# A three-layer kernel with eight experts: row sorts, weight chunks and an overflow count in second layers, and another order at the turn to the transform

## The chip, the cores and the metric

The kernel runs on one core of one Trainium2 chip. The metric is the device time of one execution in microseconds. A core has five engines with a queue each: TensorE (PE, with PEld for weight loads), VectorE (DVE), ScalarE (ACT), GpSimd (POOL) and SyncE (SP), which here only issues transfers; semaphores order the engines against each other.

## The reference, cut to what matters

```python
attn = _attn_ref(x, a, B, C)            # chunked scan, (4, 8, 768, 32)
x = attn.transpose(0, 2, 1, 3).reshape(4, 768, 256)
# _moe_ref: each token goes to one expert e, the last one or the best new one
h = np.maximum(x[b, s] @ w1[e], 0.0)    # 256 -> 1024
out[b, s] = p[e] * (h @ w2[e])          # 1024 -> 256
# _moe2_ref
mixed = np.real(np.fft.fft(np.fft.fft(x, axis=1), axis=2))
u = x + mixed
un = (u - u.mean(-1)) / np.sqrt(var + 1e-06)
return u + np.maximum(un @ w_ch1, 0.0) @ w_ch2   # 256 -> 1024 -> 256
```

All is float32; matrices are multiplied as three products of a high and a low part (`w1h`, `w1l`, `xh`, `xl`, `hh`, `hl`).

## The kernel before, in words

The program has three parts on one core. The scan and the choice of experts come first, and scatter each token's row into `xs_buf`, sorted by expert. Then come the experts, and last the transform: mixing (a Fourier transform as matmuls) and a channel layer of six groups of 512 rows, g0 to g5.

The function `experts` runs the experts in order of their load: E0 to E5, then E6 and E7. `CAPS` gives the rows that each may hold (128 and 256 for E0, then 480, 448, 384, 352, 320, 416, 416). E6 and E7 are split by batch, so that the transform can start early: of E6 the first 288 rows run, then the first 128 of E7, then the other 288 rows of E7 (hooks `rest`) and at last the other 128 of E6 (hooks `turn`). For this the rows of E6 and E7 are sorted by batch in an earlier expert: `sort_rows` loads the rows as `xu` (L981), marks and counts those in front (`tk`, `lead`, the scan `ahead`) on DVE, has TensorE add the counts up (`ps`, L1018), computes the targets (`to`, `di`) on DVE, and GpSimd scatters the rows to `xs_part` in four transfers (L1045). The sort of E6 (the first) runs within E1, that of E7 (the second) within E2; `xu` has one buffer.

`moe_expert` runs one expert: a first layer of eight steps f of six matmuls (L911), ScalarE's `hh` (L917) and DVE's `hl` (L918) after each; three PSUM buffers, so that TensorE can be three steps ahead of `hl`. The second layer runs by tiles of 128 rows (L953), or for some row counts in two halves `d` with results `yt` that are transposed back later (L944). Results are scaled on ScalarE (`y`, L1065) and scattered by token to `y_tok` on GpSimd (L1066). After every step the function calls `hook(i)`: 0 to 7 in the first layer, 8 to 11 in the second (for two halves: 8 and 10 within them, 9 and 11 behind them). In the hooks stands all work that is prepared for later:

- `load_w`/`pieces` load the weights of expert e + 2 in two transfers (`r1`, `r2`, L180 and L186) and split them, w1 on ScalarE (`w1h`, L202) and DVE (`w1l`, L205), w2 alike. The table `AT` says in which hooks the next piece is taken, `MORE` where the next load is issued.
- `prep_steps(c)` loads a chunk of the channel weights (`rawc`, L127 or L133) and converts it: four operations on DVE (L143 to L146), `c1h` or `c2h` on ScalarE (L150), two subtractions and additions on GpSimd (L152, L153). The table `PREP` holds for each chunk c the hook of its load and that of its conversion.
- `rounds` counts overflow (eight small DVE operations), and the table of the square root is loaded on ScalarE (L1174).

Everything is recorded in program order under a manual schedule, so the place of a hook is the place in the queue of each engine, and a waiting instruction holds what stands behind it. `r1`, `r2` and `rawc` share two staging buffers; a transfer waits until what was in its buffer has been read.

The transform's matmuls per batch are `stage_a` (`f`, L1350), `correct` (`cps`, L1391), `stage_b` (`mix`, L1408 and L1409); then the rows are added (`add_rows`, L1425), mean and deviation taken (`stats`, `mean`), the mean subtracted (`less`, L1466 on ScalarE or L1468 on DVE), and `split_n` transposes them (L970) for the channel layer. `fold` (L1294 to L1313) prepares a batch for `stage_a` on DVE and GpSimd. `nyquist` collects a column of three batches on GpSimd (the copies of L1363) for their joint correction. `load_z` (L1260) and `load_k` (L1273, L1277) load a batch from `y_tok`; so they wait for its last result scatter, and a later scatter to `y_tok` waits for them.

Of the kernel before, what the change touches and what calls it, by code (L numbers as in the profile page):

```python
# [31 lines left out]
AT = {0: (1, 2, 4, 5, 8, 8), NE - 2: (3, 4, 5, 6, 8, 9)}  # L32
MORE = {0: 8, 1: 10, 2: 10}
PREP = tuple((c, (e, 6), (e, 8)) for c, e in enumerate((1, 2, 3, 4, 5)))
PREP += ((5, (NE - 2, 7), (NE - 2, 10)), (6, (1, 9), (1, 10)), (7, (2, 9), (2, 10)))
# [22 lines left out]
def tile_kernel(ctx: ExitStack, tc: tile.TileContext, io):  # L58
# [815 lines left out]
    def ffn(pools, e, xt_src, evac, hook=lambda i: None, n=CAP):  # L874
# [257 lines left out]
    def experts():  # L1132
# [24 lines left out]
        for e in range(NE):  # L1157
# [7 lines left out]
            def hook(i):  # L1165
                nonlocal nxt, ws, nr
                if e in (1, 2) and i == 0:
                    srt[:] = [sort_rows(pools, SORTED[e - 1])]
                    next(srt[0])
                for _ in range({1: (2, 3, 8, 8, 8, 8), 2: (4, 5, 8, 8, 8, 8)}.get(e, ()).count(i)):  # L1170
                    next(srt[0])
                if (e, i) == (3, 8):
                    sq = sm.tile([128, 1], FP32, tag="sq", name="sq", bufs=1)
                    A.activation(out=sq, in_=ident[:, 0:1], func=ACTF.Sqrt)  # L1174
                if (e, i) == (4, 2):
                    nr = rounds(sm)
# [23 lines left out]
        return (most, cur), nr  # L1200

    def homes(i, t):
# [27 lines left out]
        else:  # L1230
# [6 lines left out]
            n = NB - 1  # L1237
# [13 lines left out]
    def transform(lead):  # L1251
# [64 lines left out]
        def mid(b):  # L1316
# [5 lines left out]
            if b < 2 or all_z:  # L1322
                correct(b)
# [206 lines left out]
        most, cur = lead  # L1530
# [4 lines left out]
        def rest(i):  # L1535
            if i == 7:
                near = xp.tile([128, 4, D], FP32, tag=f"xl{NE % 2}", name="near", bufs=1)
                two = sm.tile([128, 2 * D], I32, tag="cv", name="near").bitcast(FP32)
                home["near"] = near, [two[:, D * k:D * k + D] for k in range(2)]
                load_k(0)  # L1540
                run(0, 0, 3)
                run(0, 1, 3)

        def turn(i):
            nonlocal nxt
            if i == 0:
                stage_a(0, 1)
                correct(0)
# [5 lines left out]
                for k in range(1, 5):  # L1554
# [23 lines left out]
        stage_a(0, 0)  # L1578
# [153 lines left out]
```

## Time and profile before

| | |
|---|---|
| median of 3 runs | 451.85 us (451.26 to 455.68) |
| profiled execution | 453.64 us, span 451.8 |
| mean granted clock of TensorE | 0.977 |
| TensorE busy | 407.9 us, 90%, 3101 instructions |
| DVE, ScalarE, GpSimd busy | 62%, 42%, 35% |
| chain that ended last | PE 63%, DVE 14%, DMA 10%, ACT 7% |

The span runs from the first to the last instruction of the profiled execution; its own time beside it is measured from outside. The granted clock is TensorE's share of full speed. The chain is followed back from the last instruction to what released it.

### The profile page before, as it was taken

What the parts mean: (1) busy time and instruction counts of PE and PEld (TensorE: products, weight loads), DVE (VectorE), ACT (ScalarE), POOL (GpSimd) and SP (SyncE); (2) the same over time, 40 slices, a digit from 0 to 9 for tenths busy, and PEclk for the clock granted to TensorE, in tenths of its full rate; (3) what the DMA queues carried; (4) which work ended last, traced back from release to release, by engine and by line L of the source; (5) the groups of instructions that cost most, each with busy time, mean ns of one, the idle gap of its engine ahead of it and who ended that gap; (6) DMA issues with size and microseconds to landing.
All of it is one profiled execution on the core that took longest, in us unless ns stands there. A gap on an engine that the chain in (4) does not pass through costs nothing.

```text
span 451.8 us, 8296 instructions
## 1 busy us (share of the span) xinstructions
PE 407.9 (90%) x3101; PEld 357.8 (79%) x3101; DVE 279.7 (62%) x761; ACT 187.6 (42%) x411; POOL 158.3 (35%) x214
## 2 busy tenths in 40 slices
PE   8899888899779796969999998959999999999995
PEld 4576666498579686969999897849889898998985
DVE  5688798755456584567667385675646576754341
ACT  3455465335613624553556526413332443432230
POOL 2256876331007537240531514544402341400000
PEclk9999999999969998997999999989999999999999
DMA  8796545228814838371754140440302000010101
GB/s 286 259 311 225 165 127 150 78 82 292 267 54 137 269 85 257 123 236 65 268 169 140 39 139 25 152 143 0 118 10 79 31 32 16 15 36 13 35 13 41
DMA packets 34089, 56.26 MB, mean 125 GB/s; under 512 B 3318, under 2 KB 23063, under 8 KB 34040
## 3 DMA queue, kind: packets, MB, share of 16 engines
q1 hardware_dynamic: 30328, 46.82, 32.5%
q0 software_dynamic: 3200, 8.54, 5.5%
q8 instruction: 26, 0.43, 0.4%
q10 hardware_dynamic: 512, 0.28, 0.2%
q14 instruction: 23, 0.19, 0.1%
HBM read 42.60 MB, written 13.17 MB: 123 GB/s over the span
## 4 chain that ended last, share of the span: by engine, by line
PE 63%; DVE 14%; DMA 10%; ACT 7%; issue 3%; POOL 1%; SPq 1%; ACTq 0%; DVEq 0%
PE mm L911 21%; PE mm L953 16%; PE mm L929 6%; DMA xu<-xs_buf 3%; PE tl L517 3%; PE tp L970 3%; PE f L1350 2%; DMA rawc<-in_wc_dram 2%; DMA xn<-xs_buf 2%; DVE mt L441 2%; DVE hl L918 2%; PE g L433 2%; PE mb L281 2%; DMA home<-y_tok 2%; DVE w2l L205 1%
## 5 line engine op out<-in xcount | busy, mean ns | idle before, releaser
L918 DVE SCALAR_TENSOR_TENSOR hl<-mm,hh 128x512 fp32r<-128x512 f32 (+7 forms) x112 | 65.5, 592 | 47.1 <-ACT hh L917 47.0
L917 ACT ACTIVATE hh<-mm 128x512 fp32r<-128x512 f32 (+7 forms) x112 | 57.2, 519 | 76.3 <-PE mm L911 76.2
L911 PE MATMUL mm<-xh,w1h 128*128 128x288 f32 (+6 forms) x128 | 44.8, 357 | 13.6 <-DVE hl L918 8.2
L953 PE MATMUL mm<-c2h,hh 128*128 128x256 f32 x192 | 54.5, 284 | 0.4 <-DVE o L1490 0.4
L953 PE MATMUL mm<-c2h,hl 128*128 128x256 f32 x192 | 53.7, 279 | 0.0
L953 PE MATMUL mm<-c2l,hh 128*128 128x256 f32 x192 | 53.6, 279 | 0.0
L1066 POOL DMA_INDIRECT y_tok<-y,ids x26 | 26.6, 1023 | 46.9 <-ACT y L1065 38.1
L911 PE MATMUL mm<-xh,w1l 128*128 128x288 f32 (+6 forms) x128 | 42.8, 341 | 0.0
L911 PEld LDWEIGHTS mm<-xh,w1h 128*128 128x128 f32 x128 | 25.6, 200 | 18.4 <-DVE hl L918 11.2
L911 PE MATMUL mm<-xh,c1h 128*128 128x512 f32 x96 | 39.2, 408 | 0.0
L911 PE MATMUL mm<-xh,c1l 128*128 128x512 f32 x96 | 38.0, 395 | 0.0
L953 PEld LDWEIGHTS mm<-c2h,hh 128*128 128x128 f32 x192 | 36.1, 188 | 0.7 <-DVE o L1490 0.6
L953 PEld LDWEIGHTS mm<-c2l,hh 128*128 128x128 f32 x192 | 36.1, 188 | 0.1
L953 PEld LDWEIGHTS mm<-c2h,hl 128*128 128x128 f32 x192 | 36.1, 188 | 0.0
L441 DVE TENSOR_TENSOR mt<-g,ca 128x512 f32<-128x512 f32 x48 | 31.4, 677 | 4.6 <-PE g L433 4.2
L911 PE MATMUL mm<-xl,w1h 128*128 128x288 f32 (+6 forms) x128 | 32.7, 337 | 0.0
L911 PE MATMUL mm<-xl,c1h 128*128 128x512 f32 x96 | 29.9, 392 | 0.0
L205 DVE TENSOR_TENSOR w2l<-r,w2h 128x1024 fp32r<-128x1024 f32 (+1 forms) x18 | 21.4, 1198 | 12.9 <-ACT w2h L202 12.7
L638 POOL DMA_INDIRECT xs_buf<-scr,si x24 | 24.5, 1020 | 13.2 <-issue 5.1
L1490 DVE SCALAR_TENSOR_TENSOR o<-mm,ve,home 128x256 f32<-128x256 f32 x24 | 11.6, 484 | 27.3 <-PE mm L953 27.2
L205 DVE TENSOR_TENSOR w1l<-r,w1h 128x512 fp32r<-128x512 f32 x32 | 22.2, 698 | 9.9 <-ACT w1h L202 9.8
L953 PE MATMUL mm<-w2h,hh 128*128 128x256 f32 (+1 forms) x96 | 26.5, 286 | 0.1
(333 smaller groups left out, 1002.1 us busy)
## 6 DMA issues: line engine op xcount, KB each, us to landing
r<-in_w_dram SPq DMA_DIRECT2D x16, 1024.0 KB
rawc<-in_wc_dram SPq DMA_DIRECT2D x8, 512.0 KB
out_dram<-o SPq DMA_DIRECT2D x24, 128.0 KB
home<-y_tok SPq DMA_DIRECT2D x3, 768.0 KB
xs_buf<-scr SPq DMA_DIRECT2D x8, 265.0 KB
c1h<-in_x_dram SPq DMA_DIRECT2D x4, 512.0 KB
c2h<-in_bt_dram SPq DMA_DIRECT2D x6, 256.0 KB
c2l<-in_bn_dram SPq DMA_DIRECT2D x6, 256.0 KB
```

The costliest lines, as they stand in the source:

```text
L205: V.tensor_tensor(out=l_[:, x:y], in0=r_[:, x:y], in1=h[:, x:y], op=ALU.subtract)
L441: V.tensor_tensor(out=m[:, :, 2 * q:2 * q + 2, :], in0=gp[q], in1=cc("cmask").unsqueeze(1).unsqueeze(1).to_broadcast([128, 2, 2, 128]), op ...
L517: PE.matmul(out=tl[:, 128 * g:128 * g + 137], lhsT=x1t[:, g, u, :], rhs=ca[:, o:o + 137], start=(g == 0), stop=(g == 1), skip_group_check= ...
L638: w = G.indirect_dma_start(out=xs_buf, out_offset=bass.IndirectOffsetOnAxis(ap=si[:, b:b + 1], axis=0), in_=x1n[:, b0 + b, 0:RW], in_offse ...
L911: PE.matmul(out=ps[:, 0:n], lhsT=w[:, d, f * 128:(f + 1) * 128], rhs=x[:, d, 0:n], start=(k == 0), stop=(k == 5))
L917: A.activation(out=hf, in_=ps[:, 0:n], func=ACTF.Relu)
L918: V.scalar_tensor_tensor(out=hl[:, f, 0:n], in0=ps[:, 0:n], scalar=0.0, in1=hf, op0=ALU.max, op1=ALU.subtract)
L929: PE.matmul(out=ps[:, 0:n], lhsT=w[:, f, 128 * d:128 * d + 128], rhs=h[:, f, 0:n], start=(k == 0), stop=(k == 23),)
L953: PE.matmul(out=ps[0:m, :], lhsT=h[:, f, t * 128:t * 128 + m], rhs=w[:, f, :], start=(k == 0), stop=(k == 23))
L970: PE.transpose(ps[d][:, t * 128:(t + 1) * 128], src(t, d), ident)
L1066: w = G.indirect_dma_start(out=y_tok, out_offset=bass.IndirectOffsetOnAxis(ap=ids[0:m, t:t + 1], axis=0), in_=y[0:m, :], in_offset=None, b ...
L1490: V.scalar_tensor_tensor(out=o, in0=ps, scalar=st_[b]["rs"][:, k:k + 1], in1=st_[b]["u"][:, k].rearrange("p t d -> p (t d)"), op0=ALU.mult ...
```

## The change

It puts the sorts' steps, the chunk conversions, the split of w2, the overflow count and the table load into other hooks, and writes the turn in another order:

- Both pieces of w2 are split at hook 8 (8 and 9 before); chunks are converted at hook 9 behind them. E2 takes its w1 pieces one hook later.
- Chunk 7 leaves E2 (and so ScalarE's queue ahead of E2's `yt`); it is loaded in E6 and converted in `rest`, hook 0.
- The steps of both sorts move from first layers (hooks 2 and 3, 4 and 5) to hooks 8, 9 and 10, by the table `SORT`.
- The table load moves from E3 to E1, the overflow count within E4 to hook 8.
- In the turn, `stage_a(0, 0)` moves into `rest`, hook 10, with another buffer for its result; E7's last results (`flush`) and the load of batch 1 come ahead of correction and mixing; the mean is subtracted on DVE right behind its computation; a new hook 12 within the second layer of 128 rows holds `split_n(0)`.
- Batch 1 is corrected by itself as batch 0 is; `nyquist` collects batches 2 and 3 only, in group 1 instead of group 0.

```diff
-AT = {0: (1, 2, 4, 5, 8, 8), NE - 2: (3, 4, 5, 6, 8, 9)}
+AT = {0: (1, 2, 4, 5, 8, 8), 2: (2, 3, 4, 5, 8, 8), NE - 2: (3, 4, 5, 6, 8, 8)}
...
+PREP += ((5, (NE - 2, 7), (NE - 2, 9)), (6, (1, 9), (1, 10)), (7, (NE - 2, 9), None))
+SORT = {(1, 8): 2, (1, 9): 1, (1, 10): 3, (2, 8): 2, (2, 9): 1, (2, 10): 3}
...
+                if n == 128 and k == 11:
+                    hook(12)
             evac(t, ps[0:m, :], m)
             hook(8 + t)
...
-                for _ in range({1: (2, 3, 8, 8, 8, 8), 2: (4, 5, 8, 8, 8, 8)}.get(e, ()).count(i)):
+                for _ in range(SORT.get((e, i), 0)):
                     next(srt[0])
-                if (e, i) == (3, 8):
+                if (e, i) == (1, 9):
                     sq = sm.tile([128, 1], FP32, tag="sq", name="sq", bufs=1)
                     A.activation(out=sq, in_=ident[:, 0:1], func=ACTF.Sqrt)
-                if (e, i) == (4, 2):
+                if (e, i) == (4, 8):
                     nr = rounds(sm)
                     next(nr)
-                if (e, i) == (4, 8):
+                if (e, i) == (4, 10):
                     nr = next(nr)
-                at = AT.get(e, (1, 2, 3, 4, 8, 9))
+                at = AT.get(e, (1, 2, 3, 4, 8, 8))
...
-            n = NB - 1
+            n = NB - 2
             home["xw"], home["w"] = part(3, 1024, 6, n), part(3, 1088, 6, n)
...
-            if b < 2 or all_z:
+            if b < 3 or all_z:
                 correct(b)
...
-            if part and (b == 0 or all_z):
+            if part and (b < 2 or all_z):
                 r0, r1 = st_[b]["r"]
                 w = st_[b]["d"] = sm.tile([128, 6, 1], FP32, tag="w", name="w", bufs=4)
                 V.tensor_tensor(out=w, in0=r1[:, :, 0:1], in1=r0[:, :, 0:1], op=ALU.subtract)
             r = st_[b]["r"][part]
-            dst = home["pt", part, b % 2]
+            dst = home["pt", part, b % 2] if b or part or all_z else home["pt0"]
...
             for b in range(n):
-                G.tensor_copy(out=x[:, :, b], in_=st_[1 + b]["z"][:, :, 1, 0])
+                G.tensor_copy(out=x[:, :, b], in_=st_[2 + b]["z"][:, :, 1, 0])
...
         def rest(i):
+            if i == 0:
+                next(late)
+            if i == 10:
+                stage_a(0, 0)
             if i == 7:
...
             if i == 0:
                 stage_a(0, 1)
+                flush()
+                load_z(1)
                 correct(0)
                 for k2 in range(4):
                     stage_b(0, k2)
...
                     if k > 1:
                         mean(0, k - 2)
+                        less(0, k - 2, V)
                 mean(0, 3)
-                flush()
-                load_z(1)
+                less(0, 3, V)
                 load_k(1)
-            if i == 4:
-                for k in range(3):
-                    less(0, k, A)
-                less(0, 3, V)
+            if i == 12:
                 nxt = split_n(0)
                 residual(0, 5)
                 residual(0, 4)
...
-        stage_a(0, 0)
         moe_expert(pools, last - 1, *most, turn, n=CAPS[last - 1] - n6, t0=3)
...
-                if (g, i) in ((0, 3), (0, 4), (0, 5)):
+                if (g, i) in ((1, 3), (1, 4), (1, 5)):
                     next(nyq)
```

How this stands in the engines' queues, at three places. First DVE in the first layer of E1, before:

```order
L918 SCALAR_TENSOR_TENSOR hl<-mm_1772,hh 128x480
L995 SCALAR_TENSOR_TENSOR tk<-xu,out_of 128x4
L1009 TENSOR_SCALAR lead<-tk 128x4
L205 TENSOR_TENSOR w1l<-r_1734,w1h 128x512
L918 SCALAR_TENSOR_TENSOR hl<-mm_1786,hh 128x480
L1012 MEMSET ahead 128x1
L1013 SCALAR_TENSOR_TENSOR ahead<-cb,lead 128x4
```

DVE in the second layer of E1, now, where `ce` and `cv` are chunk 0 and `pos` waits for TensorE's `ps`:

```order
L998 SCALAR_TENSOR_TENSOR tk<-xu,out_of 128x4
L1012 TENSOR_SCALAR lead<-tk 128x4
L1015 MEMSET ahead 128x1
L1016 SCALAR_TENSOR_TENSOR ahead<-cb,lead 128x4
L206 TENSOR_TENSOR w2l<-r_1736,w2h 128x1024 x2
L1024 COPY pos<-ps 128x5
L1026 COPY nlead<-pos 128x1
L144 TENSOR_SCALAR ce__1932<-rawc 128x512
L145 SCALAR_TENSOR_TENSOR cv<-rawc,ce__1932 128x512
L146 TENSOR_SCALAR ce__1932<-cv 128x512
L147 SCALAR_TENSOR_TENSOR cr<-rawc,ce__1932 128x512
L1029 SCALAR_TENSOR_TENSOR to<-cb,nlead,pos 128x4
```

The operation that waits for `xu` moved from between two `hl` of the first layer to behind the layer's last one, and the targets `to` of the scatters moved behind chunk 0's conversion.

TensorE at the turn, where `f`, `cps` and `mix` are batch 0's mixing and L944 transposes E7's results, before:

```order
L1350 MATMUL f<-fa,home 128x128 x12
L1391 MATMUL cps<-w,fa 128x1 x6
L1408 MATMUL mix<-fb,home 128x129
L1409 MATMUL mix<-fb,home 128x128
L1408 MATMUL mix<-fb,home 128x129
L1409 MATMUL mix<-fb,home 128x128
L1408 MATMUL mix<-fb,home 128x129
L1409 MATMUL mix<-fb,home 128x128
L1408 MATMUL mix<-fb,home 128x129
L1409 MATMUL mix<-fb,home 128x128
L944 MATMUL tp<-ca,yt 128x128 x4
L944 MATMUL tp<-ca,yt 32x128 x2
```

and now:

```order
L1353 MATMUL f<-fa,home 128x128 x6
L945 MATMUL tp<-ca,yt 128x128 x4
L945 MATMUL tp<-ca,yt 32x128 x2
L1394 MATMUL cps<-w,fa 128x1 x6
L1411 MATMUL mix<-fb,pt 128x129
L1412 MATMUL mix<-fb,home 128x128
L1411 MATMUL mix<-fb,pt 128x129
L1412 MATMUL mix<-fb,home 128x128
L1411 MATMUL mix<-fb,pt 128x129
L1412 MATMUL mix<-fb,home 128x128
L1411 MATMUL mix<-fb,pt 128x129
L1412 MATMUL mix<-fb,home 128x128
```

E7's transposes moved from behind the mixing to ahead of the corrections, and six of the `f` matmuls moved into the expert ahead.

GpSimd at the turn, where `y_tok` are result scatters and L1425 (now L1428) adds the mixed rows, before:

```order
L1066 DMA y_tok<-y,ids 3072x256 x4
L1277 DMA near<-y_tok,rix 128x256 x2
L1425 TENSOR_TENSOR home<-near,a 128x256
L1426 TENSOR_TENSOR home<-near,a 128x1
L1425 TENSOR_TENSOR home<-near,a 128x256
L1426 TENSOR_TENSOR home<-near,a 128x1
L1425 TENSOR_TENSOR home<-near,a 128x256
L1426 TENSOR_TENSOR home<-near,a 128x1
L1066 DMA y_tok<-y,ids 3072x256 x3
L1277 DMA home<-y_tok,rix 128x256 x2
```

and now, from the same result scatters on:

```order
L1069 DMA y_tok<-y,ids 3072x256 x4
L153 TENSOR_TENSOR ce__3192<-cv,c2h 128x512
L154 TENSOR_TENSOR c2l<-ce__3192,cr 128x512
L1280 DMA near<-y_tok,rix 128x256 x2
L1069 DMA y_tok<-y,ids 3072x256 x3
L1428 TENSOR_TENSOR home<-near,a 128x256
L1429 TENSOR_TENSOR home<-near,a 128x1
L1428 TENSOR_TENSOR home<-near,a 128x256
L1429 TENSOR_TENSOR home<-near,a 128x1
L1428 TENSOR_TENSOR home<-near,a 128x256
L1429 TENSOR_TENSOR home<-near,a 128x1
L1280 DMA home<-y_tok,rix 128x256 x2
```

Three result scatters moved ahead of six additions, and chunk 7's two operations (L153, L154) now stand ahead of the loads.

## Rows read from the trace of the kernel before

**Rows 1.** Windows: bounds, us; busy PE, PEld, DVE, ACT, POOL; PEclk, DMA share, GB/s

```profile
112.97:144.04 31.07, 25.45 (x158) 22.89 (x157) 17.37 (x39) 12.99 (x21) 7.23 (x6) 0.89 0.45 144
144.04:168.67 24.63, 21.49 (x108) 18.84 (x107) 16.17 (x35) 10.50 (x18) 12.40 (x11) 1.00 0.59 186
168.67:193.27 24.60, 20.44 (x135) 19.64 (x134) 13.15 (x24) 11.58 (x23) 11.74 (x10) 0.93 0.59 179
193.27:216.87 23.60, 19.45 (x104) 18.51 (x103) 16.26 (x32) 11.28 (x20) 7.75 (x6) 0.86 0.49 157
216.87:248.57 31.70, 30.97 (x223) 29.96 (x221) 21.96 (x39) 20.00 (x39) 10.70 (x9) 1.00 0.57 196
286.56:309.96 23.40, 18.58 (x99) 15.63 (x97) 15.33 (x42) 7.76 (x18) 9.05 (x23) 0.93 0.38 127
```

**Rows 2.** Chain of work that ended last: start us, us, what

```profile
126.83 4.80 PE mm L911 x12
...
256.79 6.32 PE mm L911 x48
...
272.51 1.23 PE cps L1391 x12
```

**Rows 3.** Waits of TensorE: us in total, times, longest us

```profile
PE mm L911 <- DVE hl L918: 8.2, 9, 2.1
PE mm L911 <- DVE ahead L1012: 5.0, 1, 5.0
PE tp L944 <- ACT yt L935: 3.9, 1, 3.9
...
PE f L1350 <- POOL home L1308: 3.0, 1, 3.0
...
PE tp L970 <- ACT home L1466: 2.0, 1, 2.0
PE f L1350 <- DVE home L1310: 1.7, 1, 1.7
```

**Rows 4.** Timeline of SyncE's queue: start us, us, what

```profile
141.25 0.38 SPq L133 DMA_DIRECT2D rawc<-in_wc_dram  x1
...
151.03 0.37 SPq L981 DMA_DIRECT2D xu<-xs_buf  x1
...
194.47 0.37 SPq L180 DMA_DIRECT2D r<-in_w_dram  x1
```

**Rows 5.** Timeline of DVE, in E1 and E2: brackets give idle time and releaser

```profile
138.89 0.42 DVE L143 TENSOR_SCALAR ce__1922<-rawc 128x512 int32<-128x512 int32 x1
...
145.80 1.29 DVE L143 TENSOR_SCALAR ce__1996<-rawc 128x512 int32<-128x512 int32 x1 [2.53 <-DMA rawc<-in_wc_dram]
...
159.06 0.16 DVE L995 SCALAR_TENSOR_TENSOR tk<-xu,out_of 128x4 int32<-128x4 int32 x1 [3.73 <-DMA xu<-xs_buf]
```

**Rows 6.** Timeline of GpSimd, in E1 and in g0

```profile
137.84 1.98 POOL L1045 DMA_INDIRECT xs_part<-xu,di  x1 [0.77 <-DVE out_of L237]
...
142.92 1.19 POOL L1045 DMA_INDIRECT xs_part<-xu,di  x1 [0.30 <-issue]
144.12 1.31 POOL L152 TENSOR_TENSOR ce__1922<-cv,c1h 128x512 f32<-128x512 f32 x1
...
291.60 1.24 POOL L1066 DMA_INDIRECT y_tok<-y,ids  x1 [3.39 <-ACT hh L917]
...
301.59 0.19 POOL L1363 COPY home<-home 128x6 f32<-128x6 f32 x1 [2.49 <-DMA home<-y_tok]
```

**Rows 7.** Line L1045, the eight scatters of the sorts: DMA issue to landing

```profile
DMA to landing us min/median/max: 3.4/5.0/7.4
```

**Rows 8.** Timeline of ScalarE, in E3 and E4

```profile
173.86 0.63 ACT L150 ACTIVATE c2h<-cv 128x512 fp32r<-128x512 f32 x1 [5.79 <-DVE cv L144]
174.40 0.53 ACT L935 ACTIVATE yt<-mm 128x448 f32<-128x448 f32 x1
...
199.35 1.06 ACT L202 ACTIVATE w1h<-r 128x1024 fp32r<-128x1024 f32 x1 [3.12 <-DMA r<-in_w_dram]
```

More of the change, by code (lines that the diff above doesn't have):

```diff
@@ L30 @@
 CP, CT = 128, 129
-AT = {0: (1, 2, 4, 5, 8, 8), NE - 2: (3, 4, 5, 6, 8, 9)}
-MORE = {0: 8, 1: 10, 2: 10}
-PREP = tuple((c, (e, 6), (e, 8)) for c, e in enumerate((1, 2, 3, 4, 5)))
-PREP += ((5, (NE - 2, 7), (NE - 2, 10)), (6, (1, 9), (1, 10)), (7, (2, 9), (2, 10)))
+AT = {0: (1, 2, 4, 5, 8, 8), 2: (2, 3, 4, 5, 8, 8), NE - 2: (3, 4, 5, 6, 8, 8)}
+MORE = {0: 8, 1: 10}
+PREP = tuple((c, (e, 6), (e, 9)) for c, e in enumerate((1, 2, 3, 4, 5)))
+PREP += ((5, (NE - 2, 7), (NE - 2, 9)), (6, (1, 9), (1, 10)), (7, (NE - 2, 9), None))
+SORT = {(1, 8): 2, (1, 9): 1, (1, 10): 3, (2, 8): 2, (2, 9): 1, (2, 10): 3}
 FT = (
@@ L1166, in hook @@
                 nonlocal nxt, ws, nr
-                if e in (1, 2) and i == 0:
+                if (e, i) in ((1, 0), (2, 4)):
                     srt[:] = [sort_rows(pools, SORTED[e - 1])]
                     next(srt[0])
-                for _ in range({1: (2, 3, 8, 8, 8, 8), 2: (4, 5, 8, 8, 8, 8)}.get(e, ()).count(i)):
+                for _ in range(SORT.get((e, i), 0)):
                     next(srt[0])
-                if (e, i) == (3, 8):
+                if (e, i) == (1, 9):
                     sq = sm.tile([128, 1], FP32, tag="sq", name="sq", bufs=1)
                     A.activation(out=sq, in_=ident[:, 0:1], func=ACTF.Sqrt)
-                if (e, i) == (4, 2):
+                if (e, i) == (4, 8):
                     nr = rounds(sm)
                     next(nr)
-                if (e, i) == (4, 8):
+                if (e, i) == (4, 10):
                     nr = next(nr)
-                at = AT.get(e, (1, 2, 3, 4, 8, 9))
+                at = AT.get(e, (1, 2, 3, 4, 8, 8))
                 for _ in range(at.count(i) if more else 0):
@@ L1199, in experts @@
                 most = cur
-        return (most, cur), nr
+        return (most, cur, chunk[7]), nr
     def homes(i, t):
@@ L1357, in nyquist @@
         def nyquist():
-            n = NB - 1
+            n = NB - 2
             x, t, w = home["xw"], home["tw"], home["w"]
-            st_[1]["d"] = w
+            st_[2]["d"] = w
             for b in range(n):
-                G.tensor_copy(out=x[:, :, b], in_=st_[1 + b]["z"][:, :, 1, 0])
+                G.tensor_copy(out=x[:, :, b], in_=st_[2 + b]["z"][:, :, 1, 0])
             yield
@@ L1385, in correct @@
             w = st_[b]["d"]
-            n = NB - 1 if b and not all_z else 1
+            n = NB - 2 if b > 1 and not all_z else 1
             cps = pst.tile([128, 4, n], FP32, tag="tp", name="cps")
@@ L1528, in transform @@
             return
-        most, cur = lead
+        most, cur, late = lead
         last = NE - 1
@@ L1538, in rest @@
                 two = sm.tile([128, 2 * D], I32, tag="cv", name="near").bitcast(FP32)
+                home["pt0"] = sm.tile([128, 4 * 128], I32, tag="cv", name="pt").bitcast(FP32)
+                home["pt0"] = home["pt0"].rearrange("p (a b) -> p a b", a=4)
                 home["near"] = near, [two[:, D * k:D * k + D] for k in range(2)]
```

## Prediction

> **What bounds the kernel now.** I read the page first: TensorE is busy 90% of the span, no other engine above 62%, and the chain that ended last is TensorE for 63%. So the time is TensorE's work, plus the places where it stands still, plus what the clock takes after that. The next view is the six stretches [rows 1]: the experts E1, E2, E3, E4, then E5 with the leading rows of E6, and the first layer of the first channel group (g0). Each loses between nothing and 8 us against its own work at full speed. For that work I take the 48 matmuls of 288 columns in 6.32 us [rows 2], 0.457 ns a column, and scale by columns: 10.5 us for 48 matmuls of 480 columns, 9.8 for 448, 8.4 for 384, 7.7 for 352, 11.2 for 512, 2.8 for a tile of 24 with 256 columns; small matmuls of 128 columns or fewer take 0.10 each (12 in 1.23, [rows 2]). The waits of TensorE [rows 3] then say who ended each loss. After the wait of 5.05 us in E1 twelve matmuls take 4.80 us instead of 2.6 [rows 2], and the granted clock of that stretch is 0.89; E2, with a wait of 2.1, has 1.00 [rows 1]. So a long wait is paid twice here: the engine fell from 2.4 to 1.2 GHz behind it.
>
> **E1, gain 7.2.** DVE stood at `tk`, the sort's first operation, until the rows xu had landed; the `hl` behind it frees the PSUM buffer that TensorE wants (5.0, [rows 3]). The sort's steps move behind the first layer, so this wait goes: 5.0 and 2.2 of clock. The stretch holds 22.6 us of work (10.5, four tiles of 2.8, transposes), so 31.07 has 8.5 to give; the 1.3 left are small stalls that nothing here touches.
>
> **E2, loss 1.4.** The 2.1 behind `hl` [rows 3] and smaller waits go: chunk 6's load was issued when chunk 0's conversion had ended (141.25, [rows 4]) and landed 4.55 later [rows 5]; now its buffer is free after the weight split, some 3 us sooner. But the second sort pays. Its load of xu waits until the first sort's four scatters have read xu, and these now stand on GpSimd behind chunk 0's two operations (1.3 each, 144.12 in [rows 6]) and a result scatter. By order: E1's second layer begins at 125.0 instead of 132; the split of w2 (two pieces behind tile 0) ends about 131.8; the conversion takes 2.4 more (138.89 in [rows 5] to 141.25 in [rows 4]), ten small DVE operations 1.7; GpSimd is through chunk 0 and the result scatter at 138.9. So the scatters start at 138.9 where they started at 137.84, though the expert runs 7 us ahead. The last starts 5 later, 143.8 (137.84 to 142.92 in [rows 6]), and lands 5.0 (median) to 7.4 after that [rows 7]; I take 6.8, because the last one is followed by xu at 151.03 [rows 4]. xu is issued at 150.6. It landed 8.0 after its issue before (151.03 to 159.06, [rows 4, 5]), with two other loads in the two us ahead of it; now it goes alone, so I take 4.7 from the 512 KB of chunk 6 (4.55) for its 530 KB. Rows at 155.3, the scan done at 155.9. TensorE reaches the sort's matmul, which now stands between the halves of E2's second layer, at 136.8 + 0.7 + 9.8 + 4.9 = 152.2. A new wait of 3.7, between none (scatters landing in 3.4) and 7.1 (xu in 8.0), and 1.5 of clock after it, between nothing as behind 2.1 and 2.2 as in E1. 20.3 of work, 0.5 of small stalls and 5.2 make 26.0 against 24.63.
>
> The row for such a scatter is 3.4 to 7.4 us to landing [rows 7]. The Trainium skill ("DMA: Bandwidth & Descriptors", section "Anatomy of one DMA — SWDGE (gpsimd) path") fits 2.0 us plus bytes over 436 GB/s; an estimate from this is 2.3 for 136 KB and 3.2 for 530 KB. By that rule xu would be there before TensorE asks; the trace does not agree with it at these places, and the same page of the Trainium skill calls the completion of a write to HBM a surprisingly long delay.
>
> **E3, gain 6.0.** Chunk 7's `c2h` stood on ScalarE ahead of E2's results `yt` and waited 5.79 for the conversion (173.86, 174.40 in [rows 8]); TensorE waited 3.9 for yt [rows 3] with a clock of 0.93. Chunk 7 leaves this place. Work is 8.4 + 8.4 + 1.5 = 18.3 of 24.60; I leave 0.3 standing.
>
> **E4, gain 6.5.** The hl waits here are part of the 8.2 [rows 3]. ScalarE's first w1h waits 3.12 for a load issued at 194.47 that lands 4.88 later [rows 4, 8], because chunk conversions held the staging buffer. With both w2 pieces at one hook and the conversion behind them the buffer comes free some 3 us earlier in the layer. Work is 15.4 + 0.6 = 16.0 of 23.60, I keep 1.1 as a shorter wait for that load. The table load and the overflow count only change place on ScalarE and DVE, which are idle half of the stretch.
>
> **E5 and E6, gain 0.7.** TensorE is busy 30.97 of 31.70 [rows 1]; no more is there.
>
> **E7's rest, loss 1.5.** Chunk 7 is now converted behind its first `hl`: 2.4 on DVE, and c2h on ScalarE ahead of the second `hh`. Three PSUM buffers carry TensorE over three steps of 0.8 at 288 columns, so it stops at the fifth; between 0.5 and 2.5, and a wait under 2.1 costs no clock.
>
> **Turn, gain 1.9.** TensorE waits 2.0 for the centred rows [rows 3]; subtracting the mean right behind each mean on DVE, and the transposes of E7's results ahead of the mixing, take that away with 0.5 of slow transposes; the mixing may wait 0.6 for a PSUM tile.
>
> **g0, gain 6.4, less 1.2.** The first 1.7 and 3.0 of the f matmuls [rows 3] go back to GpSimd: its fold stands behind the copies that wait for the loads of batches 2 and 3 (2.49 before the one at 301.59, [rows 6]). These copies now come in the next group, and the load of batch 1 is issued some 5 us sooner. Work is 11.2 + 2.5 + 1.2 + 1.5 = 16.4 of 23.40; 0.6 stays. The price is another set of 12 correction matmuls in group 2: 1.23 [rows 2].
>
> **The sum.** 7.2 - 1.4 + 6.0 + 6.5 + 0.7 - 1.5 + 1.9 + 6.4 - 1.2 = 24.6. The profiled execution took 453.64 around its span of 451.8; less 24.6 it is 429.0. The median lies 1.8 lower, so 427.2; I say 427. About 1% (4.5 us) is what a measurement of this kernel can tell from no change.
>
> **Rivals.** *The second sort's rows come in time.* If the scatters land in their minimum of 3.4 and xu in 4.55, no wait is left in E2: 5.2 better, 422. Against it stand the 7.4 and the 8.0. The Trainium skill's rule named above would give this too. 0.15.
>
> *Weights late.* The loads of E3 to E6 are now asked for by faster experts, in the same bytes, at a DMA share of 0.59 already [rows 1]. If each lands at 7.4 instead of 4.9, four experts wait 2.5 each at their first split: 437. For it: the xu load took 8.0 in company. 0.25.
>
> *The turn gives nothing.* The last result scatter stands on GpSimd ahead of the fold and runs only at 291.60 [rows 6]; it must also wait until the loads of batch 1 have read their rows. If that holds the fold as long as the copies did, g0 keeps its waits and only the 0.5 of clock improves: 6.5 to 7 worse, 434. 0.12.
>
> *Slower.* Experts that run closer together also put their loads on top of each other. From a landing of about 8 us for all of them, five experts would each wait 3.0 and pay 2.2 of clock, 26 in all, and the gain is gone; at 10 us it is 5 x (5.1 + 2.2) = 36, 463. Only one load of the trace shows 8.0, so 0.03.
>
> **Chances and range.** The forecast has 0.45. From 419 (the first rival, with E7's wait gone too) to 439 (weights late, with the 2 us more that the upper bound of E2 gives) about 0.8 is held. All cases but the last lie more than 1% below: faster 0.95, same 0.02, slower 0.03.
>
> **What would show it.** In the profile after: in E1 no wait of TensorE for `ahead` and a clock near 1; in E2 one wait of 2 to 7 us at `ps`, and GpSimd's scatters behind chunk 0; no wait for `yt` in E3; a wait near 1 in E4 at the first hl; a wait of about 1.5 at the fifth step of E7's rest; no f matmul of g0 waiting for GpSimd over 1 us. I am wrong if E2's wait is below 1 or above 8, if weights are waited for in E5 or E6, or if g0 still takes over 20 us.

## The result, and the profile after

The changed kernel took 432.77 us (median of 4, 429.65 to 436.09), the kernel before 451.56 beside it (4 runs, 449.92 to 455.68): a ratio of 0.957, with an interval of 0.948 to 0.967. Ratios here are of mean times, without executions that were slowed as a whole, so they differ a little from the ratio of the medians. The profiled execution took 429.65 with a span of 427.8 and a clock of 0.998; the sum of the prediction had given 429.0 for it. It was the fastest of the four.

The windows of the changed kernel, in the same stages as [rows 1] (E1, E2, E3, E4, E5 with E6's leading rows; then E7's rest with the turn, and g0's first layer); the columns are those of [rows 1]:

```profile
113.64:137.44 23.80, 23.22 (x159) 21.43 (x158) 18.10 (x33) 14.71 (x23) 5.18 (x5) 1.00 0.60 193
137.44:159.87 22.43, 21.21 (x109) 18.91 (x108) 18.56 (x40) 10.63 (x18) 10.08 (x10) 1.00 0.68 214
159.87:178.76 18.89, 18.75 (x136) 18.08 (x135) 12.91 (x23) 11.06 (x22) 12.83 (x12) 1.00 0.56 189
178.76:196.60 17.84, 16.44 (x104) 15.93 (x103) 13.68 (x31) 10.02 (x18) 3.83 (x4) 1.00 0.64 215
196.60:228.28 31.68, 30.96 (x222) 29.93 (x221) 22.69 (x42) 20.77 (x40) 11.05 (x10) 1.00 0.58 196
236.37:267.26 30.89, 27.96 (x208) 26.08 (x207) 20.64 (x63) 12.44 (x32) 14.48 (x20) 1.00 0.34 117
267.26:284.80 17.54, 17.02 (x99) 14.23 (x97) 13.73 (x39) 7.68 (x18) 5.84 (x8) 1.00 0.31 98
```

The rest and the turn, in a window of the kernel before:

```profile
256.63:286.56 29.93, 27.66 (x208) 26.01 (x207) 18.50 (x59) 13.55 (x34) 10.71 (x16) 1.00 0.26 80
```

Against [rows 1] that is a gain of 7.3 in E1, 2.2 in E2, 5.7 in E3, 5.8 in E4, 0.0 in E5 and E6, a loss of 1.0 in the rest and the turn, and a gain of 5.9 in g0. Behind g0's first layer 143.0 us are left (427.8 less 284.80) where 141.8 were: the loss of 1.2 for the other set of corrections. The scan ahead of E1 took 0.7 more (113.64 against 112.97). The clock is 1.00 in every window shown.

TensorE's waits in the changed kernel, answering to [rows 3] (us in total, times, longest):

```profile
PE mm L912 <- DVE hl L919: 5.0, 6, 1.4
...
PE tp L973 <- DVE hl L906: 1.3, 1, 1.3
...
PE f L1353 <- DVE home L1313: 0.5, 1, 0.5
...
PE ps L1021 <- DVE ahead L1016: 0.2, 1, 0.2
```

The waits for the scan in E1, for `yt` in E3, for the centred rows in the turn and for GpSimd's `home` in g0 are gone. New is the 1.3 for the `hl` of 128 rows in the turn; the largest single wait behind the `hl` of L919 is below 1.5.

In E2 the wait that I had priced at 3.7 is 0.2. The path to it, on GpSimd, SyncE's queue, DVE and TensorE of the changed kernel (start, us, what, idle before):

```profile
136.61 1.31 POOL L154 TENSOR_TENSOR c1l<-ce__1932,cr 128x512 fp32r<-128x512 f32 x1
...
139.36 0.98 POOL L1048 DMA_INDIRECT xs_part<-xu,di  x1 [0.30 <-DVE ce__1998 L144]
...
143.22 0.98 POOL L1048 DMA_INDIRECT xs_part<-xu,di  x1 [0.30 <-issue]
```

```profile
149.39 0.37 SPq L984 DMA_DIRECT2D xu<-xs_buf  x1
```

```profile
153.75 0.16 DVE L998 SCALAR_TENSOR_TENSOR tk<-xu,out_of 128x4 int32<-128x4 int32 x1 [2.63 <-DMA xu<-xs_buf]
```

```profile
154.46 0.36 PE L1021 MATMUL ps<-ahead,cb 128*128 128x5 f32 x2 [0.24 <-DVE ahead L1016]
```

GpSimd's scatters do stand behind chunk 0 and start at 139.36 (forecast 138.9), the last at 143.22; xu is issued at 149.39 (150.6) and used at 153.75, 4.4 later (4.7). TensorE comes to the sort's matmul at 154.2, not 152.2, for the most part because E2 begins 0.6 later, behind the longer scan stage, and stalls 1.0 behind `hl`; the sort's own scan ends at 154.3, and the matmul starts 0.24 after TensorE was free.

### The profile page after: what moved, and what is told of

It is laid out like the page before. It is cut to its first block, busy times and chain, and to the rows that moved or that the text cites. A ratio compares the mean times of both kernels' runs of the same rounds, so it can differ in the third digit from the quotient of the medians.

```text
span 427.8 us, 8320 instructions
## 1 busy us (share of the span) xinstructions
PE 401.4 (94%) x3113; PEld 352.3 (82%) x3113; DVE 279.4 (65%) x762; ACT 187.3 (44%) x409; POOL 153.9 (36%) x213
## 4 chain that ended last, share of the span: by engine, by line
PE 67%; DVE 14%; ACT 8%; DMA 6%; issue 2%; POOL 2%; SPq 0%; ACTq 0%; DVEq 0%; POOLq 0%
PE mm L912 21%; PE mm L954 18%; PE mm L930 8%; PE tl L518 3%; PE f L1353 3%; PE tp L973 2%; PE g L434 2%; DMA xn<-xs_buf 2%; PE mb L282 2%; DVE w2l L206 2%; DVE hl L919 2%; ACT w1h L203 2%; DVE mt L442 2%; PE yb L465 1%; DMA xs_part<-xu,di 1%
## 5 line engine op out<-in xcount | busy, mean ns | idle before, releaser
L919 DVE SCALAR_TENSOR_TENSOR hl<-mm,hh 128x512 fp32r<-128x512 f32 (+7 forms) x112 | 65.1, 591 | 45.8 <-ACT hh L918 45.4
L912 PE MATMUL mm<-xh,w1h 128*128 128x288 f32 (+6 forms) x128 | 42.3, 338 | 5.5 <-DVE hl L919 5.0
L912 PE MATMUL mm<-xh,w1l 128*128 128x288 f32 (+6 forms) x128 | 40.4, 323 | 0.0
L912 PEld LDWEIGHTS mm<-xh,w1h 128*128 128x128 f32 x128 | 24.1, 188 | 9.5 <-DVE hl L919 7.6
L912 PE MATMUL mm<-xl,w1h 128*128 128x288 f32 (+6 forms) x128 | 31.1, 324 | 0.0
L206 DVE TENSOR_TENSOR w1l<-r,w1h 128x512 fp32r<-128x512 f32 x32 | 23.3, 732 | 8.3 <-ACT w1h L203 8.1
L930 PE MATMUL mm<-hh,w2h 128*128 128x288 f32 (+3 forms) x80 | 26.0, 324 | 0.0
```

What stands on the lines that cost most here:

```text
L206: V.tensor_tensor(out=l_[:, x:y], in0=r_[:, x:y], in1=h[:, x:y], op=ALU.subtract)
L912: PE.matmul(out=ps[:, 0:n], lhsT=w[:, d, f * 128:(f + 1) * 128], rhs=x[:, d, 0:n], start=(k == 0), stop=(k == 5))
L919: V.scalar_tensor_tensor(out=hl[:, f, 0:n], in0=ps[:, 0:n], scalar=0.0, in1=hf, op0=ALU.max, op1=ALU.subtract)
L930: PE.matmul(out=ps[:, 0:n], lhsT=w[:, f, 128 * d:128 * d + 128], rhs=h[:, f, 0:n], start=(k == 0), stop=(k == 23),)
```

## The experiments

Edits are against the changed kernel. Each run's text on what was expected was written before it ran. Stage times are read from its profile as above.

### The changed kernel again

No edit.

> The changed kernel itself, once more: its four executions took 429.65 to 436.09 us, and the slower ones had a clock of 0.991 where the profiled one had 0.998. My theory: in the slower ones the second sort's rows land late, TensorE waits at the sort's matmul in E2 and is slow behind it, so another profile with a time of 432 or more shows E2 at 25 to 29 us instead of 22.4 with a wait of 2 to 5 at ps. Rival: the difference lies elsewhere (weights that land late in E3 to E6), E2 stays at 22.4 and another expert is 2 to 5 us longer.

428.95 us (4 runs, 428.26 to 430.47), against 453.21 before on the same chip; 0.948, interval 0.941 to 0.955. Every stage from E1 on is within 0.3 us of the first profile (E2 22.2). No execution above 431 came, so this run decides nothing on the spread.

### The first sort's scatters ahead of chunk 0

```diff
-SORT = {(1, 8): 2, (1, 9): 1, (1, 10): 3, (2, 8): 2, (2, 9): 1, (2, 10): 3}
+SORT = {(1, 8): 2, (1, 9): 4, (2, 8): 2, (2, 9): 1, (2, 10): 3}
```

> The first sort's targets and scatters come one hook earlier, ahead of chunk 0's conversion. My theory (the second sort's rows have no slack and their delay makes the slower executions): the scatters start at about 135 instead of 139.4, xu of E2 is issued 4 us sooner, no wait at ps in any execution, the median comes to 430 (429 to 431) with a spread below 2 us. Rival (the spread has another place): median 432 to 433 and a spread of 4 to 6 us as in the changed kernel, with the scatters just as early.

431.12 us (429.8 to 434.02), ratio 0.954, interval 0.947 to 0.962, not told apart from the changed kernel. xu is issued 4 us sooner and TensorE no longer waits at the sort's matmul, but it waits longer behind `hl` (2.36 against 0.97). SyncE's queue, TensorE in E2, and DVE ahead of E2's first `hl`:

```profile
145.06 0.37 SPq L984 DMA_DIRECT2D xu<-xs_buf  x1
```

```profile
143.31 0.47 PE L912 MATMUL mm<-xh,w1h 128*128 128x448 f32 x1 [2.36 <-DVE hl L919]
```

```profile
142.03 0.69 DVE L147 SCALAR_TENSOR_TENSOR cr<-rawc,ce__1998 128x512 f32<-128x512 uint32 x1 [3.73 <-POOL c1l L154]
```

The last operation of chunk 6's conversion, which stands ahead of that `hl`, waits 3.73 for GpSimd's `c1l` of chunk 0, and this now stands behind the four scatters. E2 takes 23.3 instead of 22.4. The rows came in time, and yet the median did not fall to 430 nor the spread below 2 us: my theory of the spread fell here.

### The changed kernel with five rounds, and where executions differ

No edit; run later, on the chip of the first repeat.

> The changed kernel itself beside the one before it, on the same chip, as its control: 428 to 431 by the four executions of the last time, 429.7 to 436.1 by the first four. No edit.

438.51 us, above both of the ranges that I had given, against 460.29 before beside it: 0.955, interval 0.950 to 0.961. Window of its scan, then the scan of the first profile:

```profile
0.00:122.49 122.49, 107.59 (x1092) 78.80 (x1092) 81.99 (x269) 52.27 (x134) 54.25 (x82) 0.93 0.55 182
```

```profile
0.00:113.64 113.64, 100.13 (x1092) 73.60 (x1092) 80.32 (x269) 52.25 (x134) 54.28 (x82) 1.00 0.62 196
```

The scan takes 122.5 with a granted clock of 0.93 where it took 113.6 with 1.00, in the first profile and in the first repeat; every stage behind it is within 0.2 of the first profile. So the same kernel on the same chip differs from time to time in the scan, which the change doesn't touch, and this is why a difference of 2 us is better read from the stages than from whole times. That the spread of the first four executions has the same place is not shown; only one of them was profiled.

### The sorts where they were

```diff
-SORT = {(1, 8): 2, (1, 9): 1, (1, 10): 3, (2, 8): 2, (2, 9): 1, (2, 10): 3}
+SORT = {(1, 2): 1, (1, 3): 1, (1, 8): 4, (2, 4): 1, (2, 5): 1, (2, 8): 4}
...
-                if (e, i) in ((1, 0), (2, 4)):
+                if (e, i) in ((1, 0), (2, 0)):
```

> The steps of both sorts at the hooks of before, all else as changed. My theory: DVE stands at tk again until xu has landed, E1 goes from 23.8 to 30 to 31 us with a wait of about 5 for the scan and a clock below 1 behind it, E2 from 22.4 to 23 to 25: 434.5 to 439 in all. Rival (E1's gain came from the weight splits, not from the sort): E1 stays below 26.

443.37 us in one execution, above my range; 4.3 of that are in its scan (117.9). Besides the table, the edit puts the first step of the second sort back from hook 4 to hook 0 of E2. E1 and E2, and TensorE's wait in E1:

```profile
117.91:149.04 31.13, 25.51 (x158) 23.00 (x157) 17.29 (x39) 14.58 (x23) 7.07 (x6) 0.89 0.36 111
149.04:174.31 25.27, 22.50 (x108) 20.31 (x107) 18.61 (x35) 10.69 (x18) 13.15 (x11) 0.93 0.60 193
```

```profile
131.77 0.77 PE L912 MATMUL mm<-xh,w1h 128*128 128x480 f32 x1 [5.04 <-DVE ahead L1015]
```

E1 is 31.1 again, with the same wait of 5.0 for the scan and the same clock of 0.89; E2 is 25.3. The sorts' place is worth 7.3 in E1 and 2.8 in E2, E1's part as forecast.

### Chunk 7 back in E2

```diff
+MORE = {0: 8, 1: 10, 2: 10}
...
+PREP += ((5, (NE - 2, 7), (NE - 2, 9)), (6, (1, 9), (1, 10)), (7, (2, 9), (2, 10)))
...
-            if i == 0:
-                next(late)
```

> Chunk 7 is loaded and converted in E2 as before, and no longer in E7's rest; all else as changed. My theory: c2h stands ahead of yt again, E3 goes from 18.9 to 22 to 25 with a wait of 3 to 4 at the transposes, and the 1.3 of E7's rest go, so the kernel is 2 to 5 slower than the changed one (431 to 434). Rival (E3's gain came from the other conversions and splits): E3 stays below 20 and the kernel is 1 us faster.

433.31 us. E3, E4, and the rest with the turn:

```profile
158.74:181.41 22.67, 19.11 (x136) 18.04 (x135) 17.43 (x27) 11.97 (x23) 15.17 (x14) 1.00 0.60 187
181.41:201.89 20.48, 17.85 (x104) 17.54 (x103) 13.46 (x30) 9.71 (x18) 3.84 (x4) 0.92 0.53 181
241.65:270.98 29.33, 27.68 (x209) 26.02 (x207) 18.79 (x59) 12.15 (x31) 11.95 (x18) 1.00 0.37 123
```

E3 loses 3.8, and E4 2.6 (clock 0.92), while the rest and the turn gain 1.6. By these profiles chunk 7's move gives 6.4 and costs 1.6; the 1.6 is the forecast 1.5. The wait for `yt` in E3 is 2.0, not 3 to 4; two behind `hl` (1.2 and 0.4) are beside it. That E4 loses too was in no step of mine. Its one wait is 2.6 us here and 1.4 in the changed kernel, since the load of w1 takes 6.8 us to land instead of 5.2; why it does is open, and in the run below with chunk 7 and the splits together that load takes 5.0.

### The splits of w2 and the conversions where they were

```diff
+AT = {0: (1, 2, 4, 5, 8, 8), 2: (2, 3, 4, 5, 8, 9), NE - 2: (3, 4, 5, 6, 8, 9)}
...
+PREP = tuple((c, (e, 6), (e, 8)) for c, e in enumerate((1, 2, 3, 4, 5)))
...
+                at = AT.get(e, (1, 2, 3, 4, 8, 9))
```

> The second piece of w2 at hook 9 again and chunks converted at hook 8 ahead of it, all else as changed. My theory: the staging buffer comes free about 3 us later, E4's first w1h waits for its load, E4 goes from 17.8 to 21 to 23 with half the clock somewhere, E3 and E5 lose up to 2: 5 to 8 slower. Rival (E4's gain came with chunk 7, which was the load that held the buffer): E4 stays below 19.

431.73 us. E2 takes 23.6 (1.1 more) and E4 18.8 (0.9 more); E3 and E5 don't move. E4 stays below 19, as the rival said: this edit is worth some 2 us, not the 5 to 8 that I expected of it. E4's part is not clear of chance, for in a run below whose experts are as changed ("Both as before") E4 takes 18.6 all the same.

### Chunk 7 and the splits together

> Chunk 7 back in E2, and the split of w2 at hooks 8 and 9 with conversions at 8, both as before; sorts, count and turn as changed. E4 took 23.6 before, 17.8 changed, 20.5 with chunk 7 alone put back, 18.8 with the splits alone put back. My theory: both hold the same staging buffer, so together they cost more than their sum: E4 at 23 to 24, E3 at 23 to 25. Rival: they add up, E4 at 21.4, and the other 2.2 came from the overflow count or the table load that moved.

442.31 us, 7.1 of it more than in the changed kernel in the scan (120.7 against 113.6). E2 23.9, E3 22.7, and E4:

```profile
191.07:210.99 19.92, 17.92 (x105) 17.51 (x104) 14.06 (x30) 9.67 (x18) 6.57 (x6) 0.91 0.53 175
```

They don't reinforce each other in E4, which at 19.9 is even below the 20.5 of chunk 7 alone; 3.7 of its 23.6 are still missing.

### The overflow count and the table load put back as well

```diff
-                if (e, i) == (1, 9):
+                if (e, i) == (3, 8):
                     sq = sm.tile([128, 1], FP32, tag="sq", name="sq", bufs=1)
...
-                if (e, i) == (4, 8):
+                if (e, i) == (4, 2):
                     nr = rounds(sm)
```

> As the run with chunk 7 and the splits of w2 put back, and the overflow count and the table load put back too; only the sorts, the turn and the corrections are as changed. With chunk 7 and the splits E4 took 19.9; before it took 23.6, changed 17.8. My theory: the count's eight DVE operations (1.2 us) stand between two hl of E4 while TensorE is out of PSUM buffers, and the table load delays the split of w2 by 1.3 at the end of E3: E4 at 22.5 to 24. Rival (the count and the load are hidden, as I forecast, and the sorts in E1 and E2 shift what E4 waits for): E4 at 19.5 to 20.5.

442.06 us, 6.3 more in the scan (119.9). E4 takes 21.1, between the two ranges:

```profile
189.42:210.51 21.09, 16.91 (x104) 15.92 (x103) 15.74 (x32) 11.08 (x20) 7.46 (x6) 1.00 0.53 173
```

TensorE's waits in E4 of the kernel before, then those of this run:

```profile
197.46 0.43 PE L911 MATMUL mm<-xh,w1h 128*128 128x352 f32 x1 [1.15 <-DVE hl L918]
...
201.62 0.43 PE L911 MATMUL mm<-xh,w1h 128*128 128x352 f32 x1 [1.97 <-DVE hl L918]
...
203.88 0.66 PE L911 MATMUL mm<-xh,w1h 128*128 128x352 f32 x1 [1.03 <-DVE hl L918]
```

```profile
193.61 0.43 PE L912 MATMUL mm<-xh,w1h 128*128 128x352 f32 x1 [1.15 <-DVE hl L919]
...
197.80 0.43 PE L912 MATMUL mm<-xh,w1h 128*128 128x352 f32 x1 [2.00 <-DVE hl L919]
...
200.07 0.43 PE L912 MATMUL mm<-xh,w1h 128*128 128x352 f32 x1 [1.04 <-DVE hl L919]
```

DVE between the second and the third of them, and ScalarE at the end of E3:

```profile
197.23 0.52 DVE L919 SCALAR_TENSOR_TENSOR hl<-mm,hh 128x352 fp32r<-128x352 f32 x1
197.66 0.16 DVE L1082 TENSOR_TENSOR oex<-num,cb 128x8 f32<-128x8 f32 x1
...
198.83 0.15 DVE L1094 TENSOR_SCALAR ori<-omx 128x1 int32<-128x1 f32 x1
...
199.50 0.52 DVE L919 SCALAR_TENSOR_TENSOR hl<-mm,hh 128x352 fp32r<-128x352 f32 x1
```

```profile
184.56 1.28 ACT L1177 ACT_TABLE_LOAD   x1
```

The three waits of the kernel before are back (the one of 1.97 or 2.0 is for the weight load of [rows 8]). The count stands between two `hl` from 197.66 to 198.98, ahead of the third wait. The table load stands for 1.28 on ScalarE ahead of the split of w2, on which DVE's conversion and then the first `hl` wait; everything on that path is 1.5 later against E4's start than without it, and the first wait is back. With chunk 7 and the splits alone only the one of 2.0 was there. So the count and the load, put back together, were not hidden, and cost 2.2 of waiting; E4 is only 1.2 longer for it, because its clock is 1.00 here and was 0.91 without them. What still separates 21.1 from 23.6 is the clock too: the window before has 0.86 [rows 1].

### The turn as before

```diff
-            if i == 10:
-                stage_a(0, 0)
...
                 stage_a(0, 1)
-                flush()
-                load_z(1)
                 correct(0)
...
-                        less(0, k - 2, V)
                 mean(0, 3)
-                less(0, 3, V)
+                flush()
+                load_z(1)
                 load_k(1)
-            if i == 12:
+            if i == 4:
+                for k in range(3):
+                    less(0, k, A)
+                less(0, 3, V)
                 nxt = split_n(0)
...
+        stage_a(0, 0)
```

> The turn as before the change; chunk 7, the corrections and the rest as changed. My theory: E7's rest and the turn, 30.9 in the changed kernel, become 31.4 (29.9 of before and 1.5 for chunk 7), the load of batch 1 comes some 3 to 5 us later against g0, and the f matmuls of g0 wait 1 to 2 us more: 1.5 to 2.5 slower than the changed kernel, 434 to 435. Rival (the new turn is worth nothing, all of g0's gain comes from the corrections): the same time within 0.7 us, g0 at 17.5. Second rival: g0's gain hangs on the turn alone and is lost, g0 above 21, 437.

432.69 us (431.25 to 433.97). Rest and turn 31.5 (0.6 more), g0 19.5 (2.0 more, the wait for DVE's `home` being 2.5 instead of 0.5): 2.6 by the stages. The load of batch 1 is issued 3.1 ahead of g0, 4.3 later than in the changed kernel. My theory held, with 0.1 more than its range.

### The joint correction as before

```diff
-            n = NB - 2
+            n = NB - 1
...
-            if b < 3 or all_z:
+            if b < 2 or all_z:
                 correct(b)
...
-                if (g, i) in ((1, 3), (1, 4), (1, 5)):
+                if (g, i) in ((0, 3), (0, 4), (0, 5)):
                     next(nyq)
```

> The joint correction of batches 1 to 3 in g0 as before, all else as changed. My theory: the copies for batches 2 and 3 hold GpSimd's fold again, the f matmuls of g0 wait 3 to 5 us with half the clock behind them, g0 goes from 17.5 to 21 to 23; the 12 extra matmuls go (1.2): 3 to 5 slower, 435.5 to 438. Rival (the earlier load of batch 1 made the gain): g0 stays near 17.5 and the kernel is 1 us faster, 431.5.

430.2 us (428.11 to 430.92). g0 takes 17.9, only 0.4 more, and the part behind it 141.7, 1.3 less. GpSimd in g0 of this run, whose first row is the last result scatter and the others the copies for batches 2 and 3:

```profile
269.68 1.03 POOL L1069 DMA_INDIRECT y_tok<-y,ids  x1 [2.23 <-DVE home L1435]
...
276.83 0.54 POOL L1366 COPY home<-home 128x6 f32<-128x6 f32 x1 [0.53 <-DMA home<-y_tok]
279.03 0.22 POOL L1366 COPY home<-home 128x6 f32<-128x6 f32 x1 [1.66 <-DMA home<-y_tok]
```

The copies wait 0.5 and 1.7, and no f matmul waits for them. My theory fell: by the stages the change of the corrections by itself loses 0.9. The medians don't show it (430.2 against 428.95 of the first repeat).

### Both as before

The edits of the last two runs together.

> The turn and the joint correction both as before, so that only the part on the experts is changed. With the turn alone as before g0 took 19.5, with the joint correction alone 17.9, changed 17.5 and before 23.4. My theory now: either edit by itself takes away most of the same wait, so without both g0 takes 22.5 to 24 and the kernel 436 to 439. Rival (the edits add up): 17.5 + 2.0 + 0.4 = 19.9, and the kernel 432.

433.73 us; rest and turn 31.5, g0 21.7. The window of g0, then TensorE and GpSimd in it:

```profile
268.60:290.28 21.68, 17.34 (x98) 14.43 (x97) 15.90 (x42) 7.64 (x18) 9.83 (x23) 1.00 0.38 132
```

```profile
278.26 1.70 PE L1353 MATMUL f<-fa,home 128*128 128x128 f32 x12 [2.50 <-DVE home L1313]
...
283.48 1.16 PE L1353 MATMUL f<-fa,home 128*128 128x128 f32 x8 [1.67 <-POOL home L1311]
```

```profile
273.17 1.24 POOL L1069 DMA_INDIRECT y_tok<-y,ids  x1 [2.94 <-DVE hl L919]
...
280.54 0.98 POOL L1366 COPY home<-home 128x6 f32<-128x6 f32 x1 [3.18 <-DMA home<-y_tok]
```

The waits of [rows 3] are back: 2.5 for DVE's `home` and 1.7 for GpSimd's (before 1.7 and 3.0), the second behind a copy that waited 3.2 for batch 2. The old turn alone has only the first, the old corrections alone neither. With 4.1 for both where the single ones cost 2.0 and 0.4, the edits overlap: either alone takes away the wait for GpSimd. It fell short of my range of 22.5 to 24; against the 23.4 of before the clock differs too, 1.00 here and 0.93 there.

### Three edits on top

The joint correction as before, chunk 7 converted ahead of E7's rest, and one more addition of rows on DVE:

```diff
-            if i == 0:
-                next(late)
...
-                    add_rows(0, k, G if k else V)
+                    add_rows(0, k, G if k > 1 else V)
...
         load_z(0)
+        next(late)
         moe_expert(pools, last, *cur, rest, n=CAPS[last] - n7, t0=1)
```

> The changed kernel with three edits: the joint correction of batches 1 to 3 in g0 as before; chunk 7 converted ahead of E7's rest instead of behind its first hl; and the second addition of rows in the turn on DVE instead of GpSimd. My theory: 0.8 from the correction (1.2 in the tail less 0.4 in g0), 1.3 from the wait at the fifth step of E7's rest, 1.2 from the wait for GpSimd's rows in the turn that ends in the 1.3 wait for hl: 2.5 to 3.3 faster than the changed kernel, rest and turn at 28.3 to 29. Rival: the wait for hl stays, since DVE's subtractions stand ahead of it, and chunk 7's GpSimd operations delay the load of batch 0: at most 1 us faster.

438.06 us with a scan of 125.3, beside 438.51 of the changed kernel with a scan of 122.5 on the same chip; against the kernel before 0.955, interval 0.949 to 0.960. Whole times don't tell the two apart. Rest with turn, and g0:

```profile
247.74:276.38 28.64, 27.71 (x209) 26.07 (x207) 19.85 (x62) 12.54 (x32) 13.88 (x18) 1.00 0.38 126
276.38:295.19 18.81, 17.47 (x98) 14.38 (x97) 15.28 (x43) 7.64 (x18) 7.95 (x19) 1.00 0.28 91
```

The rest and the turn take 28.6 (2.3 less, as expected) and the part behind g0's first layer 141.7 (1.2 less), but g0 takes 18.8, 1.3 more. Of these 0.4 are the correction's, as above. For the rest, a shorter turn brings g0 closer to the loads that it needs: the load of batch 1 is issued 6.6 ahead of g0 (7.4 in the changed kernel), the last result scatter runs 1.9 into it (1.0), the parts of the fold on GpSimd and DVE behind that end 0.9 later, and an `hl` behind them makes TensorE wait 0.5. The wait of 1.3 at the fifth step of E7's rest is gone and the one in the turn is 0.65; which of the edits brings how much was not taken apart. From E1's start to the end it is 311.5 (436.8 less 125.26) against 314.0 (436.5 less 122.49): about 2.5 us, well under 1%, seen in one profile of each.

## Why the prediction was right, and where it was not

**The total** is right: 24.6 forecast, 24.0 between the two spans (451.8 less 427.8). The median of 432.77 lies within the range of 419 to 439; by medians the gain is 18.8, and 24.3 and 21.8 in the two repeats. That the sum comes so close to the two spans is luck: E2 came out 3.6 better than its term, and E3, E4, E5 with E6, the rest and turn, g0 and the scan together 4.3 worse than forecast.

**E1** (7.2 forecast, 7.3 measured) is right in mechanism and size: with the sorts back, the wait of 5.0 and the clock of 0.89 return.

**E2** is wrong in sign: a loss of 1.4 forecast, a gain of 2.2 measured, with a wait at `ps` of 0.24, which lies below the 1 that I had named as a sign of being wrong. The step that failed is the difference of two times: the scan's end at 155.9 and TensorE's arrival at 152.2. Each end was off by some 2 us (154.3 and 154.2), and the wait of 3.7 was their difference. The queue behind chunk 0 that I had found is there; the scatters start 3.9 from first to last instead of 5, and xu is issued 6.2 after the last instead of 6.8. With the wait, the 1.5 of clock behind it fell away too. The other step, that the wait of 2.1 behind `hl` goes, held by half: 0.97 is left. The rival "rows come in time" had the sign right, but not by its condition, a landing of 3.4 for the scatters; the wait is gone in good part because TensorE came later.

The Trainium skill ("DMA: Bandwidth & Descriptors", section "Anatomy of one DMA — SWDGE (gpsimd) path") has a fit for transfers that GpSimd issues; the estimate from it was 2.3 for a scatter and 3.2 for xu, which SyncE issues. The runs do not agree, with 2.7 to 6.9 to landing for the scatters and 4.4 for xu in the changed kernel.

**E3** (6.0, 5.7): right in size, and in the main in mechanism: chunk 7 in E2 brings 3.8 of it back. There the wait for `yt` is 2.0 with a clock of 1.00, not 3.9 with 0.93 as before; where the other 1.9 come from was not traced.

**E4** (6.5, 5.8): the size is right, the reason only in part. I put it on the staging buffer that comes free sooner, and called the overflow count and the table load free. The load of w1 is indeed issued sooner, 1.1 ahead of E4 instead of 1.2 behind its start (194.47 in [rows 4] against 193.27):

```profile
177.67 0.37 SPq L181 DMA_DIRECT2D r<-in_w_dram  x1
```

That is 2.3 sooner, where I had said some 3, and the wait for it fell from 1.97 to 1.4. But the count and the load bring two waits of 1.1 each back, and with the table load back that issue is 1.2 behind E4's start again. The step "only change place on ScalarE and DVE, which are idle half of the stretch" failed: the count lay between two `hl` while TensorE was out of PSUM buffers, and the table load ahead of the split and the conversion that free the staging buffer. The splits by themselves are worth at most 0.9 here, chunk 7's place 2.6 with its clock in one profile. The rest is the clock (0.86 before), which no run put back in full; what brought it down stays open.

**E5 and E6** (0.7, 0.0): the 0.7 of idle time is still there; no edit reached it.

**E7's rest** (loss of 1.5): right, a wait of 1.31 at the fifth step, and 1.6 back with chunk 7 in E2. TensorE in the changed kernel:

```profile
241.01 0.40 PE L912 MATMUL mm<-xh,w1h 128*128 128x288 f32 x1 [1.31 <-DVE hl L919]
```

**The turn** (gain 1.9) was over-sized. Against the old turn it gains 0.6: the wait of 2.0 for ScalarE became one of 1.3 for DVE, whose `hl` now stands behind all four subtractions, and these behind GpSimd's additions, which stand behind the result scatters that were moved ahead.

**g0** (6.4, 5.9): the size is right, the reason for the most part not. I put the gain on the copies that leave g0, and only named the load of batch 1, which comes 4.4 sooner (some 5 forecast). The rows of SyncE's queue before, then of SyncE's queue and of GpSimd in the changed kernel, show what moved:

```profile
283.53 0.36 SPq L1260 DMA_DIRECT2D home<-y_tok  x1
...
294.32 0.95 SPq L1260 DMA_DIRECT2D home<-y_tok  x2
```

```profile
259.85 0.36 SPq L1263 DMA_DIRECT2D home<-y_tok  x1
...
270.73 0.95 SPq L1263 DMA_DIRECT2D home<-y_tok  x2
```

```profile
268.22 1.03 POOL L1069 DMA_INDIRECT y_tok<-y,ids  x1 [2.24 <-DVE home L1435]
```

The load of batch 1 is issued 7.4 ahead of g0 (259.85 against 267.26; 3.0 before, 283.53 against 286.56). The last result scatter, which writes the tensor that this load reads, runs 1.0 into g0 (268.22; 5.0 before, [rows 6]), and the loads of batches 2 and 3 are issued 3.5 into it (270.73; 7.8 before, 294.32). So the copies would find their rows nearly in time where they were (waits of 0.5 and 1.7 in the run with the joint correction as before, and none of TensorE behind them). I had seen that order in a rival, as a reason for a loss, and not that an earlier load also pulls the scatter and the next loads. The price of 1.2 for the extra corrections is right, and buys 0.4 in g0 with the new turn (17.9 to 17.5); with the old turn it would have bought 2.2 (21.7 to 19.5).

## What to carry to other kernels

A wait forecast as the difference of two arrival times is no better than the worse of them: give it both signs unless the gap is larger than their errors. And a sum that comes out right says little of its terms: here one term was 3.6 off and the others made up for it. Small operations are free only away from the instruction that hands a buffer back: eight operations of 0.16 us between two such instructions cost TensorE a microsecond in a stretch where DVE was idle a third of the time. When two edits each remove the same wait, measure them apart: by the stages one of them here is a net cost.

## What the runs showed of the hardware that was not expected

A wait's length alone did not decide the clock. In E4, with chunk 7 and the splits put back, a single wait of 2.0 was followed, six matmuls later, by about ten matmuls of 352 columns at 0.29 us a step (1.2 GHz; window clock 0.91). A single wait of the same length left the clock at 1.00 in two other runs (1.98 with the splits alone put back, 2.00 with the turn and the correction as before), and with the count and the load put back too, waits of 1.15, 2.0 and 1.04 left the step at 0.16 (2.4 GHz; window clock 1.00); the kernel before, with the same three, fell to 0.29 behind the last. So the prediction's "a wait under 2.1 costs no clock" does not hold in general. What decides between them stays open.
